# Block attention with two gated layers on one core: keys of half the batch laid side by side, two pairs' means added by a product, a new table of ranks

## The chip, the cores and the metric

The kernel runs on one core of a Trainium2 chip. The metric is the device time of one execution in microseconds. Three runs of the kernel before took 600.68, 600.81 and 597.73 us (median 600.68). One more execution was profiled; it took 599.21 us, of which 597.5 us lie between its first and last instruction (the span).

## The reference

Attention of 2 batches, 8 heads, 768 positions and head size 64, and behind it two feed-forward layers over the 1536 rows of 512 columns. A query sees the keys less than 16 positions away, and beside them 24 block scores: its product with the elementwise maximum of each block of 32 keys, plus ln 32. Both kinds share one softmax; the block weights are multiplied with the block means of the values.

```python
k_sum = k.reshape(B, H, nb, block, D).max(axis=3)      # block = 32, nb = 24
v_sum = v.reshape(B, H, nb, block, D).mean(axis=3)
scores_l = where(|i - j| < 16, scale * q @ k.T, -1e9)
scores_s = scale * einsum('bhsd,bhnd->bhsn', q, k_sum) + log(block)
a = softmax(concat([scores_l, scores_s]))
attn = a @ concat([v, v_sum], axis=2)
x = attn as 1536 x 512
x = (silu(x @ w_gate) * (x @ w_val)) @ w_out           # 512 -> 1536 -> 512
h = x @ w_in                                           # 512 -> 2048
g = where(h >= 1, h, where(h <= -1, 0, (h + 1)**2 / 4))
out = g @ w2_out
```

The weights arrive as 64-bit numbers and are decoded on the chip into 32-bit ones.

## The kernel before, in words

**Order.** No loop fixes the order of the work. The program registers all work as jobs, each with the engines it may run on and an assumed cost on each, a rank, the jobs it needs, and the buffers it takes and gives back. A planner (`Plan.emit`) picks again and again the job with the smallest start plus weighted rank, on the engine that looks cheapest, and emits its instructions. The table `T` holds ranks, leads, and a weight for each kind of engine. So a change of any number in `T`, or of an assumed cost, may move instructions everywhere. Each engine runs its instructions in the order they were emitted, and the loads and stores stand in one line on SP's queue. Where the planner expects TensorE to wait, `bank` puts up to 14 dummy transposes of the identity ahead of the job (L315, below called pads).

**Attention.** Rows are in three chunks of 512: chunk 0 is batch 0, positions 0 to 511; chunk 1 the rest of batch 0 and the first 256 rows of batch 1; chunk 2 the rest. Heads go in pairs (4 pairs, two heads on the two halves of the partitions), positions in segments of 256, each of 4 tiles of 64 queries. A tile's scores have 120 columns: 96 keys around it and 24 block maxima. For batch 0 the steps of a pair are:
- `kp` (L541): keys are transposed by products with the identity, into two banks (80 and 64 partitions, 16 of them twice).
- `kt` (`kprep_out`): four copies put each tile's 96 keys into `kwin`, one window beside another, overlaps written twice. `km` (`kmax`): block maxima by two reductions on DVE. `kc` (`kmax_out`): the 24 maxima are copied behind each of the 12 windows.
- `sc` (L660): 8 products of 64 queries with 120 columns for each segment. They go to four quarters of the array in turn (which head: row half; which tile of two: column half).
- `mx` (L673, mask and maximum), `ex` (L685, on ACT), `su`/`iv`, `no` (L698, on DVE or POOL), `wt` (L706, transposes into `pt`), `pt` (copied into `pT`).
- `vm` (L509): products of values with a small averaging matrix give the block means in `pv`; `vo` copies them, `ve` (`vmean_put`) copies them on 24 partitions behind each window's values in `vall`, for 8 windows at a time in batch 0.
- `av` (L611): 16 products for each segment, `vall` window (120 rows) by `pT`, into `px`; `xh` copies it on (`x`, rounded), `xl` holds the rest (`px` less `x`).

**Weights.** Columns of w_gate and w_val come in packs of two blocks (`load`); `high` (L917) and `low` on ACT or DVE, `bits` (L926, `wb`), `hi` (`wA`, rounded) and `lo` (L956, the rest) decode a pack. The first products need the first pack and `x`, `xl` of pair 0.

**Products.** Each product of the layers is three passes over high and low parts (`mm3`, L1017): `pg`, `pv`, `acc_y` and `pi` of chunk 0, then `qg`, `qv`, `ro`, `qi`, `rz` for chunks 1 and 2 together, in a seven-product form with sums of blocks made by DVE, or by accumulating DMAs on POOL's queue (`SWD`). The last group of `rz` (p = 4) fills two banks `u` of two column halves `z`; the first half of each is copied and stored as soon as it is done, and the planner keeps writes to the second half behind that copy.

Of the kernel before, what the change touches and what calls it, by code (L numbers as in the profile page):

```python
# [25 lines left out]
 'urge': 0.00011346069898928726,  # L26
 'weight': (1.02, 5246.192, 0.325, 0.246),
# [3 lines left out]
 'd': (7426.952, -4102.226),  # L31
 'load': (-416.392, 5468.45),
 'high': (-5467.851, 6761.982),
 'bits': (-4632.926, 1843.592),
 'keep': (-308.073, -3352.145),
 'read': -1167.652,
 'hi': (-17420.635, 2225.546),
 'lo': (-17088.659, -5268.44),
 'head_rank': (-7078.75, -1117.711, -15102.701, -541.927),
 'half_rank': -3059.895,  # L40
 'start': 318.124,
 'unit': 0.87,
 'e0': 435.229,
 'a1': (61.823, 20.151),
 'a2': (189.329, 3.57),
 'x': (-4041.441, 6543.658),
 'first': (-854.098, 2600.892),
 'st_q': (-1384.045, -839.14),
 'st_qt': (1837.901, 4589.592),
 'st_sc': (-5614.707, -2280.841),  # L50
 'st_mx': (-1948.611, -5245.124),
 'st_ex': (4545.125, -695.61),
 'st_iv': (-4062.65, -3165.785),
 'st_no': (3318.58, 1959.608),
 'st_wt': (-144923.789, -442.806),
 'st_pt': (3747.761, 1508.611),
 'st_av': (-5559.373, -4379.57),
 'st_xh': (4195.107, -5.4),
 'st_xl': (-1026.525, -5190.027),
 'kl': (-9172.661, -250.396),  # L60
 'kp': (2952.663, -4662.355),
 'kt': (-2213.424, 261.921),
 'km': (-2717.732, -11590.452),
 'kc': (4577.0, 14734.269),
 'vl': (2791.992, 4670.201),
 'vm': (4107.362, 3808.015),
 'vs': -7497.287,
 'vo': (2313.603, -25934.416),
 've': (1052.554, 4976.716),
 'ql': (-5577.219, -14715.322),  # L70
 'wl': (-2275.937, -19196.435),
 'wide': 4,
 'st_su': (-668.269, 6285.357),
 'seg': (-3459.658, 407.411),
 'ko': (1505.985, 573.628),
 'swd': -3.45,
 'edge': 2,
 'j': 8901.273,
 'jus': 84.768,
 'cap': (19.368, 86.309),  # L80
 'lead': (3.861, 6.562, -15.754, -44.079, 30.375, -21.312, -1.156, -7.677, -5.803, 8.813, 1.459, -43.099, -0.913, 10.89, 0.906, 0.905, -35.721, 38.133, 2.844, 42.453, 40.532, -82.313, 14.043, -46.999, -71.2, 1.812)}


class Plan:
# [17 lines left out]
    WEIGHT = dict(zip(("ACT", "DVE", "DVE+", "POOL", "SWD"), (*T["weight"], T["swd"])))  # L102
# [33 lines left out]
    def emit(self):  # L136
# [14 lines left out]

        def free_at(ring, more=0):
            n = len(used[ring]) + more - self.rings[ring]
            if n < 0:
                return 0.0
            t, left = used[ring][n] if n < len(used[ring]) else (0.0, 1)
            return None if left else t

        while ready:
            best = None  # L160
            for name in ready:
# [15 lines left out]
                for kind, us in engines.items():  # L177
                    engine, port = kind.strip("+"), kind == "POOL" or kind[-1] == "+"
                    start = max(start0, free.get(engine, 0.0))
# [28 lines left out]
            idle = start - free.get(engine, 0.0)  # L208
            free[engine] = start + us
# [39 lines left out]
def tile_block_attention_ffn(  # L249
# [266 lines left out]

    def vmean_put(b, p, i, engine):
# [8 lines left out]
    PARTS = ((0, 80, ((0, 1), (1, 6))), (64, 64, ((7, 4), (11, 1))))  # L526

    def kprep(b, p, *tags):
        n = S // P
        for i, (r0, rows, _) in enumerate(PARTS):  # L530
# [14 lines left out]
    def kprep_out(p, i, engine):  # L545
        pk = pend["pk", p, i]
        r0, _, groups = PARTS[i]
# [9 lines left out]
    def kmax(p):  # L557
        n = PARTS[0][1] * (S // P) // BLOCK
        for i, at, to in ((0, 0, n), (1, n, NB)):
            col = at * BLOCK - PARTS[i][0] * (S // P)  # L560
            nc.vector.tensor_reduce(
                kmaxs[p][:, at:to],
# [37 lines left out]
    def values(c, p, tag, one=None):  # L600
# [3 lines left out]
        for i, (b, s) in enumerate(chunk_segments(c)):  # L604
            if one not in (None, i):
                continue
            pT, vwin = pend.pop(("pT", b, s, p)), vwins[(b * NSEG + s) % 2]
            for w in range(WPS):
                col = i * SEG + w * QT
                for h in range(2):  # L610
                    nc.tensor.matmul(  # L611
                        px[h * D:(h + 1) * D, col:col + QT], vwin[0:KN, w, 2 * p + h],
                        pT[0:KN, 2 * h + w // 2, w % 2 * QT:(w % 2 + 1) * QT],
                        start=True, stop=True,
                    )
# [22 lines left out]
    def stages(b, s, p, wide, first=None):  # L638
# [4 lines left out]
        def scores(*tags):  # L643
# [12 lines left out]
            for w in range(0, WPS, 2):  # L656
                for j in range(2):
                    for h in range(2):
                        head = slice(h * D, (h + 1) * D)
                        nc.tensor.matmul(  # L660
                            scs[h][j * QT:(j + 1) * QT, w // 2],
                            qT[head, (w + j) * QT:(w + j + 1) * QT], kwin[p][head, s * WPS + w + j],
# [57 lines left out]
        ("sc", {"PE": 0.57}, "st_sc", ()),  # L720
# [4 lines left out]
        ("no", {"DVE+": 0.67, "POOL": 1.25}, "st_no", ("iv",)),  # L725
# [5 lines left out]
    def head_jobs(b, p, t, banks, after):  # L731
# [5 lines left out]
        job(("kl", *n), {"DMA": (0.95, 1.65 if b else 1.8, 2) if near else (0.45, 1.55, 1)}, t + T["kl"][b], lambda e, ring: load_k(b, p, ring), (), (("kraw",) if near else ("kraw", "kord"),),  # L737
            after=after)
        keys = ("kl", *n)
        job(kp, {"PE": 0.78 if near else 1.95}, t + T["kp"][b], lambda e, *tags: kprep(b, p, *tags[:2]),  # L740
            [keys] + before, (banks, banks), [(keys, 0)])
        for i, us in enumerate(((0.87, 0.92), (0.69, 0.75))):
            job(("kt", *n, i), dict(zip(("ACT", "DVE"), us)), t + T["kt"][b],
                lambda e, i=i: kprep_out(p, i, e), [kp], (), [(kp, i)])
        job(("km", *n), {"DVE": 0.97}, t + T["km"][b], lambda *_: kmax(p), [kp], (),
            [(kp, 0), (kp, 1)])
        job(("kc", *n), {"DVE+": 0.36, "POOL": 0.7, "ACT": 0.4}, t + T["kc"][b], lambda e: kmax_out(p, e), [("km", *n)] + before)
        if p == 0:
# [13 lines left out]
            job(("vo", b), {"DVE": 0.25, "ACT": 0.27}, t + T["vo"][b], lambda e: vmean_out(b, e),  # L762
                [("vm", b)], (), [(("vm", b, 0) if steps else ("vm", b), 0)])
        for i in range(2 if b else 1):
            job(("ve", *n, i), {"POOL": 0.9, "ACT": 0.62, "DVE+": 0.43} if b else {"POOL": 1.8, "ACT": 1.1, "DVE+": 0.75}, t + T["ve"][b],
# [3 lines left out]
    def step_jobs(c, p, t, banks, after):  # L769
# [4 lines left out]
        job(("ql", *n), {"DMA": (0.96 * len(pieces(c)), 1.08, 2 * len(pieces(c))) if c else (0.45, 0.9, 1)}, t + T["ql"][c > 0], lambda e, ring: load_q(c, p, ring), (),  # L774
            (("s16", "s17") if c else ("s16", "s17", "s14", "s15"),), after=after)
        job(("q", *n), {"PE": 0.42 if c else 1.0}, t + T["st_q"][c > 0], lambda e, tag, _: queries(c, p, tag),
            [("ql", *n)], (banks, ("qT",)), [(("ql", *n), 0)])
        job(("qt", *n), {"DVE": 0.7, "ACT": 0.61}, t + T["st_qt"][c > 0],
# [13 lines left out]
        if not c:  # L792
            for i, (b, s) in enumerate(segs):
                u = t + T["seg"][0] * i
                h = (*n, i)
                job(("av", *(h if not i else n)), {"PE": 0.56},
                    u + T["st_av"][0], lambda e, tag, i=i: values(c, p, tag, i),
                    [("pt", b, s, p), ("ve", b, p, 0), ("wl", b, s)] + ([("av", *n, 0)] if i else []), (banks,),
                    [(("wt", b, s, p), 1)])
                av, xh, xl = (("av", *n), ("xh", *n), ("xl", *n)) if i else (  # L800
                    ("av", *h), ("xh", *h), ("xl", *h))
                job(xh, {"ACT": 0.4, "DVE": 0.42}, u + T["st_xh"][0],
# [27 lines left out]
    def segment_jobs(b, s, p, t, banks, done):  # L830
# [3 lines left out]
        more = {"sc": [("kt", b, p, 0), ("kt", b, p, 1), ("kc", b, p), ("qt", c, p)]}  # L834
# [14 lines left out]
        for name, engines, dt, needs in STAGES:  # L849
            fn = fns[name]  # L850
            if name == "su" and not wide:
                continue
# [938 lines left out]
```

## Time and profile before

| what | value |
|---|---|
| runs | 597.73, 600.68, 600.81 us |
| profiled execution | 599.21 us, span 597.5 us |
| TensorE (PE) busy | 586.8 us, 98% |
| VectorE (DVE) busy | 488.5 us, 82% |
| ScalarE (ACT) busy | 397.8 us, 67% |
| GpSimd (POOL) busy | 107.7 us, 18% |
| share of PE in the chain that ended last | 91% |

PE's busy time counts everything it runs, pads too, and ends of products are modelled; so a window in which PE is all busy may still hold a few tenths lost where it changes from one kind of product to another. The other engines' busy shares say how much room each has, not what they hold up.

### The profile page before, as it was taken

How to read it: one execution, taken by the hardware profiler on the slowest of the kernel's cores; microseconds unless marked ns; L12 is line 12 of the kernel's file. 1: busy time of each engine (PE TensorE's matmuls, PEld its weight loads, DVE VectorE, ACT ScalarE, POOL GpSimd, SP SyncE). 2: the span in 40 equal slices, each digit the busy share in tenths (PEclk: the TensorE clock that was granted, in tenths of full speed). 3: DMA queues.
4: the chain of work that ended last, by engine and by line, in shares of the span. 5: the costliest groups of instructions: out<-in, count | busy, mean ns of one | idle time of the engine just before them, and what ended most of it. 6: DMA issues, size and time to landing. Idle time of an engine off the chain costs nothing.

```text
span 597.5 us, 10820 instructions
## 1 busy us (share of the span) xinstructions
PE 586.8 (98%) x3989; PEld 498.4 (83%) x3989; DVE 488.5 (82%) x885; ACT 397.8 (67%) x734; POOL 107.7 (18%) x133
## 2 busy tenths in 40 slices
PE   8889999999999999999999999999999999999997
PEld 7779888888787778888888888888788788999996
DVE  4888888998887989887877777988988899989850
ACT  4797776674887988664443436577858677887631
POOL 3221000000031110331101001361320121255000
PEclk9999999999999999999999999999999999999999
DMA  8999999998573997998978457999789698999221
GB/s 212 304 325 271 310 328 311 362 360 321 176 259 102 261 292 289 296 210 236 255 209 195 159 159 184 315 232 176 141 207 238 207 194 241 302 233 186 46 71 54
DMA packets 117429, 137.81 MB, mean 231 GB/s; under 512 B 38784, under 2 KB 94080, under 8 KB 117376
## 3 DMA queue, kind: packets, MB, share of 16 engines
q1 hardware_dynamic: 101056, 114.05, 59.8%
q0 software_dynamic: 16320, 23.07, 23.4%
q8 instruction: 31, 0.51, 0.3%
q14 instruction: 22, 0.18, 0.1%
HBM read 91.23 MB, written 28.31 MB: 200 GB/s over the span
## 4 chain that ended last, share of the span: by engine, by line
PE 91%; DMA 3%; DVE 3%; SPq 1%; ACT 1%; issue 0%; POOL 0%; POOLq 0%; DVEq 0%; ACTq 0%
PE rz L1017 14%; PE acc_y L1017 13%; PE ro L1017 10%; PE qv L1017 10%; PE qg L1017 10%; PE qi L1017 9%; PE pi L1017 8%; PE pg L1017 6%; PE pv L1017 6%; PE px L611 2%; DMA sj<-wj 2%; PE sc L660 2%; PE pt L706 1%; DMA raw<-in_moe_w_val_dram 1%; PE pk L541 1%; PE pq L592 1%
## 5 line engine op out<-in xcount | busy, mean ns | idle before, releaser
L1017 PE MATMUL rz<-wr,cells 128*128 128x256 f32 x672 | 81.4, 283 | 0.6 <-ACT ra L408 0.5
L1017 PEld LDWEIGHTS rz<-wr,cells 128*128 128x128 f32 x672 | 81.0, 192 | 1.2 <-ACT ra L408 1.0
L1017 PE MATMUL ro<-cells,wr 128*128 128x512 f32 x252 | 57.9, 390 | 0.0
L1017 PEld LDWEIGHTS ro<-cells,wr 128*128 128x128 f32 x252 | 47.2, 188 | 10.3 <-ACT ru L408 0.6
L1017 PE MATMUL acc_y<-wA,h 128*128 128x512 f32 x192 | 47.6, 395 | 0.0
L1017 PE MATMUL qi<-cells,wjs 128*128 128x512 f32 x192 | 46.3, 389 | 0.0
L1017 PE MATMUL pi<-y,wA 128*128 128x512 f32 x128 | 45.2, 405 | 0.0
L956 DVE TENSOR_TENSOR wA<-wb,wA 128x1024 fp32r<-128x1024 f32 x34 | 42.6, 1256 | 2.4 <-ACT wA L408 1.6
L917 ACT ACTIVATE dd<-raw 128x1024 f32<-128x1024 f32 x34 | 38.8, 1145 | 7.7 <-DMA raw<-in_moe_w_val_dram 5.5
L926 DVE SCALAR_TENSOR_TENSOR wb<-dd 128x1024 int32<-128x1024 int32 x34 | 42.0, 1239 | 2.0 <-ACT dd L408 0.9
L1017 PEld LDWEIGHTS qi<-cells,wjs 128*128 128x128 f32 x192 | 36.0, 188 | 7.5
L1017 PEld LDWEIGHTS acc_y<-wA,h 128*128 128x128 f32 x192 | 35.3, 188 | 7.3 <-issue 0.2
L1017 PE MATMUL qi<-cells,wjo 128*128 128x512 f32 x144 | 35.9, 390 | 0.4 <-DVE qu L1398 0.4
L1017 PE MATMUL qg<-cells,wjs 128*128 128x512 f32 x144 | 35.6, 390 | 0.0
L1017 PE MATMUL qv<-cells,wjs 128*128 128x512 f32 x144 | 35.4, 389 | 0.0
L1017 PE MATMUL acc_y<-h,wA 128*128 128x512 f32 x144 | 35.1, 391 | 0.0
L1017 PE MATMUL pg<-x,wA 128*128 128x512 f32 (+1 forms) x112 | 34.5, 367 | 0.3 <-ACT x L408 0.3
L1017 PE MATMUL pv<-x,wA 128*128 128x512 f32 (+1 forms) x112 | 34.0, 362 | 0.0
L956 DVE TENSOR_TENSOR wjs<-sj,wjs 128x1024 fp32r<-128x1024 f32 x20 | 24.5, 1224 | 10.0 <-ACT wjs L408 9.8
L1017 PEld LDWEIGHTS qi<-cells,wjo 128*128 128x128 f32 x144 | 26.9, 188 | 6.3 <-DVE qu L1398 0.8
L1017 PEld LDWEIGHTS qg<-cells,wjs 128*128 128x128 f32 x144 | 27.0, 188 | 5.8 <-DVE wjs L956 0.2
L1017 PEld LDWEIGHTS qv<-cells,wjs 128*128 128x128 f32 x144 | 27.0, 188 | 5.6
(228 smaller groups left out, 1346.1 us busy)
## 6 DMA issues: line engine op xcount, KB each, us to landing
raw<-in_moe_w_out_dram SPq DMA_DIRECT2D x14, 1024.0 KB, 7.9
raw<-in_moe_w_in_dram SPq DMA_DIRECT2D x16, 512.0 KB, 6.6
raw<-in_moe_w_gate_dram SPq DMA_DIRECT2D x12, 512.0 KB, 7.5
raw<-in_moe_w_val_dram SPq DMA_DIRECT2D x12, 512.0 KB, 8.4
kept_g<-wb SPq DMA_DIRECT2D x12, 512.0 KB, 6.6
wj<-kept_g SPq DMA_DIRECT2D x12, 512.0 KB, 7.7
sj<-kept_g SPq DMA_DIRECT2D x24, 256.0 KB, 4.2
big<-in_v_dram SPq DMA_DIRECT2D x24, 192.0 KB, 4.8
```

Of the source, the lines that this page charges most:

```text
L541: nc.tensor.matmul(cols[h * D:(h + 1) * D, r], kraw[b, p][one, h, r], ident[one, one], start=True, stop=True, skip_group_check=True)
L592: nc.tensor.transpose(pq[:, r * P:(r + 1) * P], raw[:, r].rearrange("p h d -> p (h d)"), ident)
L611: nc.tensor.matmul(px[h * D:(h + 1) * D, col:col + QT], vwin[0:KN, w, 2 * p + h], pT[0:KN, 2 * h + w // 2, w % 2 * QT:(w % 2 + 1) * QT], s ...
L660: nc.tensor.matmul(scs[h][j * QT:(j + 1) * QT, w // 2], qT[head, (w + j) * QT:(w + j + 1) * QT], kwin[p][head, s * WPS + w + j], start=Tru ...
L706: nc.tensor.transpose(pt[0:KN, w * P:(w + 1) * P], v_["sm"][:, w], ident)
L917: nc.scalar.activation(x[:, 0], raws[k][:, :, :, 1].bitcast(F32), AF.Prelu, scale=2.0 ** -112, alpha=2.0 ** 32)
L926: nc.vector.scalar_tensor_tensor(b, x[:, 0], 3, x[:, 1], op0=ALU.logical_shift_left, op1=ALU.bitwise_or)
L956: e.tensor_tensor(out, a, b, op=ALU.subtract)
L1017: nc.tensor.matmul(dst, lhs(a), rhs(b), start=first and i == 0, stop=last and i == 2, **more)
```

## The change

Four things change, and the table of ranks with them.

1. Batch 0's keys are no longer copied into windows. `kprep_out` copies each bank's 384 columns side by side into `lines`; `kmax` writes the 24 maxima behind them, and `kc` is gone for batch 0. The two banks are 64 partitions each. A tile's scores are now two products in the same quarter of the array: 96 keys, then 24 maxima (16 products for each segment in place of 8).
2. For chunk 0 of pairs 0 and 1 (`APART`) the block means aren't copied behind the windows first. A tile `vn` (zero in its first 96 partitions, means in the next 24) is multiplied with all 256 columns of `pT` for each head, and the window products (96 rows) are added to it. `ve` for these two pairs then fills 4 windows, not 8.
3. The last `rz` products are registered as column half 0 of both banks, then column half 1 of both.
4. POOL may now also run `lo`, `gated`, `square`, sums and subtractions that were DVE's (or accumulating DMAs'); two kinds `DVE-` and `DVE=` get weights of their own. Nearly all numbers of `T` are new.

```diff
- 'weight': (1.02, 5246.192, 0.325, 0.246),
+ 'weight': (0.478, 9216.415, 0.434, 0.466, 0.153, 0.189),
...
+    def means_put(p, engine):
+        at = APART.index(p) * 2 * D
+        copy(engine, means[0][KW:KN, at:at + 2 * D], pend["pv", 0][32 * p:32 * p + NB, 0:2 * D])
+
     def vmean_put(b, p, i, engine):
-        n = WPS if b else 2 * WPS
+        n = WPS if b or p in APART else 2 * WPS
...
+    def parts_of_keys(b):
+        return ((0, 64, ()), (64, 64, ())) if b in LINE else PARTS
...
-    def kprep_out(p, i, engine):
+    def kprep_out(b, p, i, engine):
         pk = pend["pk", p, i]
+        if b in LINE:
+            copy(engine, lines[p][:, i * S // 2:(i + 1) * S // 2], pk[:, 0:S // 2])
+            return
...
+            if apart:
+                for h in range(2):
+                    at = (2 * APART.index(p) + h) * D
+                    nc.tensor.matmul(
+                        px[h * D:(h + 1) * D, i * SEG:(i + 1) * SEG], means[0][0:KN, at:at + D],
+                        pT[0:KN, 2 * h:2 * h + 2].rearrange("p x c -> p (x c)"),
+                        start=True, stop=False, skip_group_check=True)
...
+                        if b in LINE:
+                            at = wstart(s * WPS + w + j)
+                            both = ((slice(0, KW), slice(at, at + KW)), (slice(KW, KN), slice(S, S + NB)))
+                            for to_, from_ in both:
+                                nc.tensor.matmul(
+                                    to[:, to_], qs, lines[p][head, from_], start=True, stop=True,
+                                    skip_group_check=True)
+                            continue
...
-        job(("kc", *n), {"DVE+": 0.36, "POOL": 0.7, "ACT": 0.4}, t + T["kc"][b], lambda e: kmax_out(p, e), [("km", *n)] + before)
+        if b not in LINE:
+            job(("kc", *n), {"DVE+": 0.36, "POOL": 0.7, "ACT": 0.4}, t + T["kc"][b], lambda e: kmax_out(p, e), [("km", *n)] + before)
...
-        job(("lo", k), {"DVE+": COST["lo"]["DVE+"]}, t + T["lo"][late(k)], lambda e: lo_pack(k, e), [("hi", k)], (),
+        job(("lo", k), COST["lo"], t + T["lo"][late(k)], lambda e: lo_pack(k, e), [("hi", k)], (),
...
-                steps += [(p, j, x) for x in (every if st == 1 else [(y,) for x in every for y in x])
+                steps += [(p, j, x) for x in (every if st == 1 else [(every[u][z],) for z in range(2) for u in range(2)])
```

PE ahead of the first layer products, in the kernel before (`sc` scores, `pt` transposed weights of the softmax, `pv` with L509 block means, `px` attention's output, `pg` first layer; 128x128 of the identity alone is a pad):

```order
L660 MATMUL sc<-big_78,big_119 64x120 x16
L509 MATMUL pv<-big_119 32x128 x16
L509 MATMUL pv<-vrest,big_119 32x128 x8
L315 MATMUL px<-ident 128x128 x12
L611 MATMUL px<-pT,big_119 64x64 x16
L315 MATMUL px<-ident 128x128 x7
L611 MATMUL px<-pT,big_119 64x64 x16
L1017 MATMUL pg<-x_696,wA 128x256
```

Two pairs' outputs stand here with pads ahead of each, and the first `pg` right behind the second.

The same place in the changed kernel, where L639 is the product with the means and L750 the transposes:

```order
L514 MATMUL pv<-vrest,big_119 32x128 x8
L320 MATMUL px<-ident 128x128 x2
L639 MATMUL px<-pT,vn 64x256 x2
L646 MATMUL px<-pT,big_119 64x64 x8
L639 MATMUL px<-pT,vn 64x256 x2
L646 MATMUL px<-pT,big_119 64x64 x8
L639 MATMUL px<-pT,vn 64x256 x2
L646 MATMUL px<-pT,big_119 64x64 x8
L639 MATMUL px<-pT,vn 64x256 x2
L646 MATMUL px<-pT,big_119 64x64 x8
L320 MATMUL pt<-ident 128x128 x7
L750 MATMUL pt<-ident,big_78 120x128 x8
```

The four segments of pairs 0 and 1 stand together now, and 8 of the transposes of pairs 2 and 3 have moved ahead of the first `pg`.

ACT from the first pack's decoding to the copies of `px`, in the kernel before (`dd` decoding, exponentials L685, `big_119<-big_119` the copies of means behind the windows, `x` the copies of `px`):

```order
L917 ACTIVATE dd<-raw 128x1024
L685 ACTIVATE big_78<-big_78,mx 128x120 x4
L408 ACTIVATE pT<-pt 120x512 x3
L408 ACTIVATE big_119<-pv 128x128
L917 ACTIVATE dd<-raw 128x1024
L408 ACTIVATE dd<-raw 128x1024
L685 ACTIVATE sm_79,big_78<-sm_79,mx 128x120 x4
L408 ACTIVATE big_119<-big_119 24x8x128 x2
L408 ACTIVATE x_696<-px 128x256 x2
L408 ACTIVATE x_709<-px 128x256 x2
```

Both copies of means and two sets of exponentials stand ahead of the copies of `px` here.

The same place in the changed kernel (`vn` the copies of means for pairs 0 and 1):

```order
L973 ACTIVATE dd<-raw 128x1024
L413 ACTIVATE pT<-pt 120x512
L729 ACTIVATE big_78<-big_78,mx 128x120 x4
L413 ACTIVATE vn<-pv 24x128 x2
L413 ACTIVATE big_119<-pv 128x128
L413 ACTIVATE big_119<-big_119 24x4x128 x2
L973 ACTIVATE dd<-raw 128x1024
L413 ACTIVATE dd<-raw 128x1024
L413 ACTIVATE x_723<-px 128x256 x2
L413 ACTIVATE x_732<-px 128x256 x2
L729 ACTIVATE sm_79,big_78<-sm_79,mx 128x120 x4
```

Four exponentials and one copy of `pT` have left the stretch, the copies of means are halved in size, and two small copies into `vn` have come in.

## Rows read from the trace of the kernel before

**Rows 1.** The page: busy time by engine; the chain that ended last, by engine.
```profile
PE 586.8 (98%) x3989; PEld 498.4 (83%) x3989; DVE 488.5 (82%) x885; ACT 397.8 (67%) x734; POOL 107.7 (18%) x133
...
PE 91%; DMA 3%; DVE 3%; SPq 1%; ACT 1%; issue 0%; POOL 0%; POOLq 0%; DVEq 0%; ACTq 0%
```
**Rows 2.** Busy time by stretch: PE, PEld, DVE, ACT, POOL, clock, DMA share, GB/s.
```profile
30.00:60.00 30.00, 27.38 (x306) 24.76 (x305) 25.60 (x64) 26.00 (x65) 5.91 (x6) 1.00 1.05 298
60.00:90.00 30.00, 30.00 (x200) 24.41 (x199) 26.22 (x69) 21.61 (x57) 2.52 (x3) 1.00 1.05 319
...
450.00:480.00 30.00, 29.58 (x131) 24.19 (x130) 25.33 (x38) 23.17 (x37) 3.38 (x3) 1.00 0.78 204
```
**Rows 3.** PE in order of time: start, us, line, tile [idle before <-releaser].
```profile
15.43 0.23 PE L541 MATMUL pk<-ident,kord 80*64 80x80 f32 x1
15.45 0.27 PE L588 MATMUL pq<-ident,qraw 128*64 128x128 f32 x1
...
31.77 0.98 PE L315 MATMUL px<-ident 128*128 128x128 f32 x7
34.65 1.15 PE L611 MATMUL px<-pT,big 120*64 120x64 f32 x32 [1.89 <-ACT big L408]
36.14 0.39 PE L1017 MATMUL pg<-x,wA 128*128 128x256 f32 x1 [0.34 <-ACT x L408]
```
**Rows 4.** The chain that ended last, from 40 us: start, us, what.
```profile
40.35 0.87 PE pt L706 x8
...
42.81 2.02 PE px L611 x64
...
48.14 0.72 PE pg L1017 x6
...
51.45 0.57 PE sc L660 x16
```
**Rows 5.** ACT in order of time, 25 to 37 us.
```profile
25.13 1.20 ACT L917 ACTIVATE dd<-raw 128x1024 f32<-128x1024 f32 x1 [2.42 <-DMA raw<-in_moe_w_val_dram]
26.21 0.39 ACT L685 ACTIVATE big<-big,mx 128x120 f32<-128x120 f32 x1
...
27.73 1.55 ACT L408 ACTIVATE pT<-pt 120x512 f32<-120x512 f32 x3
29.16 0.28 ACT L408 ACTIVATE big<-pv 128x128 f32<-128x128 f32 x1
...
30.85 1.16 ACT L408 ACTIVATE dd<-raw 128x1024 int32<-128x1024 uint32 x1
31.91 0.38 ACT L685 ACTIVATE sm<-sm,mx 128x120 f32<-128x120 f32 x1
...
33.54 2.13 ACT L408 ACTIVATE big<-big 24x1024 f32<-24x1024 f32 x2
35.70 1.21 ACT L408 ACTIVATE x<-px 128x256 fp32r<-128x256 f32 x4
```
**Rows 6.** DVE in order of time: both halves of two packs, and `xl`.
```profile
28.35 1.22 DVE L956 TENSOR_TENSOR wA<-wb,wA 128x1024 fp32r<-128x1024 f32 x1
...
32.04 1.87 DVE L926 SCALAR_TENSOR_TENSOR wb<-dd 128x1024 int32<-128x1024 int32 x1 [0.59 <-ACT dd L408]
...
34.68 1.23 DVE L956 TENSOR_TENSOR wA<-wb,wA 128x1024 fp32r<-128x1024 f32 x1
...
36.12 1.42 DVE L628 TENSOR_TENSOR xl<-px,x 128x256 fp32r<-128x256 f32 x4
```
**Rows 7.** The end, in order of time: PE's weight loads and ACT's copies.
```profile
588.54 4.01 PEld L1017 LDWEIGHTS rz<-wr,cells 128*128 128x128 f32 x33 [0.32 <-ACT ra L408]
...
593.22 0.77 PEld L1017 LDWEIGHTS rz<-wr,cells 128*128 128x128 f32 x6 [0.68 <-ACT ra L408]
593.22 0.97 PE L1017 MATMUL rz<-wr,cells 128*128 128x256 f32 x6 [0.47 <-ACT ra L408]
```
**Rows 8.** POOL in order of time: a subtraction of the layers.
```profile
56.92 1.30 POOL L956 TENSOR_TENSOR h<-u,h 128x512 fp32r<-128x512 f32 x1
```

More of the change, by code (lines that the diff above doesn't have):

```diff
@@ new lines @@
+ 'half_rank': -424.23,
+ 'start': 559.042,
+ 'unit': 0.506,
+ 'e0': 422.878,
+ 'a1': (74.069, 21.997),
+ 'a2': (183.261, 21.332),
+ 'x': (2962.191, -6338.631),
+ 'first': (6168.202, 1133.574),
+ 'st_q': (-5550.855, -349.613),
+ 'st_qt': (-2822.789, -5933.592),
+ 'st_sc': (-4129.389, -2047.311),
+ 'st_mx': (934.53, 433.773),
+ 'st_ex': (6611.948, -5681.133),
+ 'st_iv': (-4707.567, -4306.953),
+ 'st_no': (7610.928, 2185.245),
+ 'st_wt': (-130662.294, -864.398),
+ 'st_pt': (-2099.047, 8242.495),
+ 'st_av': (3867.69, -17386.017),
@@ L100 @@
     SWITCH, LEAD, TILED = 0.11, 0.09, ("sc", "av", "kp", "vm")
-    WEIGHT = dict(zip(("ACT", "DVE", "DVE+", "POOL", "SWD"), (*T["weight"], T["swd"])))
+    WEIGHT = dict(zip(("ACT", "DVE", "DVE+", "POOL", "DVE-", "DVE=", "SWD"), (*T["weight"], T["swd"])))
     def __init__(self, rings):
@@ L150, in emit, with queue @@
         ready = [name for name in jobs if not waits[name]]
+        def queue(engine):
+            return "POOL" if engine == "SWD" else engine
         def free_at(ring, more=0):
@@ L177, in emit @@
                 for kind, us in engines.items():
-                    engine, port = kind.strip("+"), kind == "POOL" or kind[-1] == "+"
-                    start = max(start0, free.get(engine, 0.0))
+                    engine, port = kind.strip("+-="), kind == "POOL" or kind[-1] in "+-"
+                    start = max(start0, free.get(queue(engine), 0.0))
                     if engine == "DMA" or engine == "SWD":
@@ L207, in emit @@
             ready.remove(name)
-            idle = start - free.get(engine, 0.0)
-            free[engine] = start + us
+            idle = start - free.get(queue(engine), 0.0)
+            free[queue(engine)] = start + us
             if port:
@@ L607, in values @@
             pT, vwin = pend.pop(("pT", b, s, p)), vwins[(b * NSEG + s) % 2]
+            apart = not c and p in APART
+            rows_ = slice(0, KW if apart else KN)
+            if apart:
[5 more added lines that the diff above has]
+                        start=True, stop=False, skip_group_check=True)
             for w in range(WPS):
@@ L724, in tile_block_attention_ffn @@
         ("iv", {"DVE": 0.37}, "st_iv", ("ex",)),
[L725 removed]
+        ("no", {"DVE-": 0.67, "POOL": 1.0}, "st_no", ("iv",)),
         ("wt", {"PE": 0.42}, "st_wt", ("no",)),
@@ L850, in segment_jobs @@
             fn = fns[name]
+            if name == "sc" and b in LINE:
+                engines = {"PE": 0.62}
             if name == "su" and not wide:
                 continue
+            if name == "pt" and not c:
+                engines = {"ACT": 0.61, "DVE=": 0.69}
             if wide and name == "ex":
@@ L1188, in use_jobs, with act_jobs @@
                     put_jobs(c, m, t, names[m], acc, UE)
-    def act_jobs(kind, h, src, t, made, held, slots, dve="DVE"):
+    def act_jobs(kind, h, src, t, made, held, slots, inside=False):
+        dve = "DVE-" if inside else "DVE"
         gate = ("u" if h[0] in JOINT else "u2", *h)
@@ L1370, in term_jobs @@
                 lambda e, ring, b=b: term_hi(st, k, b, e, ring), [source, *before], (CELLS,))
-            job(split(b), {"DVE+": 0.7}, LATE,
+            job(split(b), {"DVE-": 0.7, **({} if b == 4 else {"POOL": 1.32})}, LATE,
                 lambda e, b=b: term_lo(st, k, b, e), [("th", st, k, b)], (),
@@ L1564, in stage_rows @@
                     [("rl", *n_)], (("wA",),), follows=prior("gh", ("wh", *n_)))
-                job(("wl", *n_), {"DVE+": cut[2]}, LATE,
+                job(("wl", *n_), {"DVE-": cut[2], **({} if p == 7 else {"POOL": cut[3]})}, LATE,
                     lambda e, a=n_, sign=sign: cut_weight(*a, sign, "lo", e), [("wh", *n_)], (),
```

196 lines of the change are left out of this document (100 added, 96 removed).

## Prediction

> **What bounds the kernel now.** I read the page's busy times and chain first. PE is busy 98% of the span, and 91% of the chain that ended last is its own [rows 1]. So time can come from three places only: work that PE does, time in which PE has nothing it may do, and the two ends. The view by stretches says where PE is idle: 27.38 of 30 are busy from 30 to 60 us, then it fills its windows (30.00); the worst one later is 450 to 480 with 29.58 [rows 2]. Over the whole product part the holes I can name come to about 1.2 us. That is all a better order could win there. The head is different. Between 28 and 37 us PE runs pads and waits: 7 pads of 0.98 us, then 1.89 us for ACT's copy of the means behind the windows (`big`), then 0.34 us for `x` [rows 3]. The first layer product starts at 36.14 us, although the first pack's rest was ready at 28.35 + 1.22 = 29.57 us [rows 6]. So 6.6 us of the head are spent on attention's chain through ACT. At the end PE's weight loads stand still twice, 0.32 and 0.68 us, for ACT's copy `ra` [rows 7].
>
> **The change part by part.**
>
> *The head.* Of ACT's work between the first pack and `x`, I price the new order by the old durations [rows 5]. It starts when the first pack lands, at 25.13 us, in both: the loads ahead of it on SP's queue are the same in number. Decoding takes 26.21 - 25.13 = 1.08, one `pT` (29.16 - 27.73)/3 = 0.48, four exponentials 27.73 - 26.21 = 1.52, two copies into `vn` 2 x 0.28. That makes 28.77 us for the means of pairs 0 and 1, on which `px` waits. Then come the copy of `pv` (0.28), two copies of means at half the size (2.13/2 = 1.06), and the second pack's two decodings (31.91 - 30.85 = 1.06 each): 32.23 us. `x` of pair 0 follows in half of 1.21, at 32.84, pair 1 at 33.44. Before, `x` began at 35.70.
>
> PE in the meantime: `px` for one segment is 32 records (a product of unrounded numbers shows as two), and 64 took 2.02 us [rows 4], so 0.50 us for a segment. The product with the means adds 4 records of 256 columns; at 2.02/64 us for 64 columns, four times that each, 0.50 us. No row shows this product itself. By columns it can't cost less than a rounded 256-column product, 0.72/6 = 0.12 us a record [rows 4], which gives 0.48, and at four times a whole 64-column segment's share it would not pass 1 us; I take 0.50. Four segments from 28.77 are done at 32.8. Behind them stand 7 pads (0.98) and 8 transposes (0.87, rows 4). The first layer product then starts at 34.7 us, not 36.14. That is 1.4 us sooner, with 8 transposes already done that stood later before: 1.4 + 0.9 = 2.3 us. Bounds: nothing, if something else is late; and 4.2 us if PE did not stand behind the pads and transposes (36.14 - 32.84, and the 0.9).
>
> What is late next is DVE. It now makes `xl` of two pairs (1.42 us from 32.9) before the second pack, whose three steps took 34.68 + 1.23 - 32.04 = 3.87 us [rows 6]: ready at 38.2 us. The first pack feeds PE for 24 half products, 24 x 0.12 = 2.9 us, until 37.6. I put 0.3 us on it (from 0 to 0.6). The head wins 2.0.
>
> *Keys and maxima.* The shorter transposes, the dropped window copies and `kc` free some microseconds of DVE and ACT before 22 us. Both then wait for the first pack (ACT idles 2.42 us before it, rows 5), so I count nothing; from 0 to 1 us gained.
>
> *Scores.* A segment's 16 records of 120 columns took 0.57 us [rows 4], 0.036 each. Now 16 of 96 and 16 of 24 run. If columns alone count, that is the same time. If a 24-column record costs as much as one of `px`'s 64-column records (2.02/64 = 0.032), it is 0.8 x 0.57 + 16 x 0.032 = 0.96, so 0.39 more. `px` has two tiles at a time and scores have four, so I halve the record: 0.8 x 0.57 + 0.25 = 0.71, 0.14 more. Eight segments lie in the head, ahead of the wait for the first pack, which covers them. Four lie among the products, where nothing does: 4 x 0.14 = 0.6 us lost (0 to 1.6). [...]
>
> *The end.* PE now turns to the other bank while ACT copies the first half. In the new order at least 6 products (0.7 us at 0.12) lie between the end of a half and the first write behind its copy, and the copy is 0.4 us long. Both waits go. PE's own rows show 0.47 for the second, the loads 0.32 + 0.68 [rows 7]; I take 0.9 (0.6 to 1.0). The last product, copy and store remain as they are.
>
> *The product part.* Attention's pieces cut the products in as many places as before (41 changes to another kind of product in either order), so nothing changes by their number. POOL takes some 27 elementwise operations more and 15 accumulating DMAs less. One costs it 1.30 us [rows 8], against 0.7 on DVE. DVE is 82% busy, POOL 18% [rows 1]; PE stood behind neither for long. A new order may lose as easily as win: between -1.2 (every hole closed) and 27 x 0.6 = 16 us (each extra on PE's path, far off). PE's full windows are the nearest row, so I take +0.3.
>
> The sum: -2.0 + 0.6 - 0.9 + 0.3 = -2.0 us. From the profiled execution's 599.21 (span 597.5, 1.7 around it) that is 597.2. This execution lies 1.5 under the median of the three runs and 0.5 under their mean (599.75). On the mean the sum gives 597.7; I forecast 597.6 us, 0.5% under the median.
>
> **Rivals.**
>
> *DVE takes the head's place.* If the second pack's rest comes 2 us later than I have it, because maxima, a copy of means and `xl` now stand ahead of it on DVE, PE waits at its 25th half product and the head gives nothing. For it: DVE's steps there stand close, and one `wb` took 1.87 us [rows 6]. Against it: the exponentials that fed those steps are done sooner. Time: 599.2 + 0.6 - 0.9 + 0.3, about 599.2, or 600.2 with half the gain at the end lost too; no change.
>
> *One tile, one turn.* Both products of a tile go to the same quarter of the array, one behind the other. If PE starts products strictly in order, the next quarter waits until the 24-column one has started, and scores no longer run four abreast. A transposition of 128 columns on the whole array takes 0.87/8 = 0.11 us [rows 4], so a record of 96 columns 0.08; 16 of them in a row are 1.3 us and the short ones hide or add 0.3: 0.75 to 1.05 us more for a segment, say 0.9. Four among the products lose 3.6. Eight in the head lose 7.2, of which the gap ahead of `px` takes some 3: 4 us late. The time is 599.2 - 2.0 + 3.0 + 4.2 = 604.4 us, slower. It decides from about 0.35 us a segment on. Against it: a `pk` record starts at 15.43, ahead of the last `pq` record at 15.45 that stands before it in the program [rows 3], so a free quarter need not wait for a busy one. [...]
>
> *The new order closes the holes.* With POOL's help DVE is never late, the head wins 3.5: 599.2 - 3.5 + 0.3 - 0.9 - 1.0 = 594.1.
>
> **How the numbers follow.** Forecast 0.50, its own range 595.5 to 599.5; DVE in the head 0.23; one tile one turn 0.15; holes closed 0.12. The whole range goes from 594.0 to 603.0: the third rival's time, and most of the second's. About 0.5% (3 us) is what runs of this kernel, 3 us apart themselves, can tell from no change. Faster than 597.7 are half of the forecast's cases, a little more for the named covers, and all of the holes': 0.28 + 0.12 + a little of the first rival's, 0.42. Slower than 603.7 is most of the second rival's and a tail for a bad order: 0.16. The rest, 0.42, is no change.
>
> **What would show it.** Right: `px` starts near 29 us, the first `pg` near 34.7, no wait of PE's loads for `ra` at the end, scores of a segment at 0.6 to 0.8 us, PE full from 60 us on. Wrong: a `sc` segment over 1.2 us; a gap of PE before its 25th half product ended by DVE `wA`; waits for POOL's `cells`, `h` or `u` in the products.

## The result, and the profile after

The changed kernel takes 604.38 us (median of 6 runs, 603.87 to 605.63), the kernel before 600.13 (median of 6, 597.73 to 600.83): a ratio of 1.0079, 95% interval 1.0058 to 1.0099. It is slower by 0.8%. The forecast was 597.6, and the range ended at 603.0. The span of the profiled execution is 602.7 us, 5.2 more than before.

The page of the changed kernel has the busy time by engine, the queue that brings instructions (packets, MB, share of 16 engines), and the chain:

```profile
PE 588.9 (98%) x4188; PEld 501.1 (83%) x4188; DVE 495.1 (82%) x872; ACT 397.9 (66%) x729; POOL 130.0 (22%) x142
...
q8 instruction: 33, 0.54, 0.4%
...
PE 88%; DVE 4%; ACT 2%; issue 2%; SPq 2%; DMA 2%; POOL 0%; ACTq 0%; DVEq 0%; POOLq 0%
```

Against [rows 1], PE's rows count 199 products more and as many weight loads; 192 of them are those of the scores that were cut in two. The chain has "issue" at 2%, before 0%: time in which an engine waited for nothing that the profile shows. The queue of instructions carried 33 packets, 31 before. What PE waited for, over the whole span (us in total, times, longest):

```profile
PE sc L701 <- issue: 4.6, 3, 2.3
PE pt L320 <- DVE xl L663: 1.0, 1, 1.0
```

The place is shown by PE in order of time, in the head (start, us, line, tile, count, idle before; a row joins neighbouring products of several shapes under the first one's shape). It answers to [rows 3]:

```profile
12.23 1.70 PE L701 MATMUL sc<-big,big 64*64 64x96 f32 x81
14.87 1.00 PE L701 MATMUL sc<-big,big 64*64 64x96 f32 x41 [0.94 <-issue]
...
18.14 0.64 PE L514 MATMUL pv<-big 96*32 96x128 f32 x14
19.12 0.84 PE L514 MATMUL pv<-big 96*32 96x128 f32 x18 [0.34 <-issue]
...
22.28 1.30 PE L701 MATMUL sc<-big,big 64*64 64x96 f32 x53
25.89 0.48 PE L701 MATMUL sc<-big,big 64*64 64x96 f32 x11 [2.31 <-issue]
...
27.31 1.09 PE L614 MATMUL pq<-ident,qraw 128*64 128x128 f32 x16
...
29.80 1.33 PE L701 MATMUL sc<-big,big 64*64 64x96 f32 x56
32.52 0.47 PE L701 MATMUL sc<-big,big 64*64 64x96 f32 x8 [1.39 <-issue]
...
33.94 0.65 PE L639 MATMUL px<-pT,vn 120*64 120x256 f32 x4
34.43 0.64 PE L646 MATMUL px<-pT,big 96*64 96x64 f32 x16
...
38.78 0.98 PE L320 MATMUL pt<-ident 128*128 128x128 f32 x7 [1.02 <-DVE xl L663]
...
40.40 0.36 PE L1073 MATMUL pg<-x,wA 128*128 128x256 f32 x1
```

Runs of scores break off in the middle: 53 products, 2.31 us of nothing, then the 11 that were left. The products behind the gap belong to the same job, and need nothing that the ones ahead of it did not need. The granted clock is 1.00 in every stretch of 5 us up to 45 us here, so the clock has no part in this execution's loss. The first layer product (`pg`) starts at 40.40 us, 36.14 before, 34.7 in the prediction. ACT, in order of time, now waits for PE where [rows 5] show it at work:

```profile
28.45 0.60 ACT L413 ACTIVATE big<-pq 128x512 f32<-128x512 f32 x1 [2.82 <-PE pq L614]
...
33.63 0.56 ACT L413 ACTIVATE vn<-pv 24x128 f32<-24x128 f32 x2 [1.54 <-PE pv L514]
```

The stretches of [rows 2], and one more, 90 to 120 us, in which PE now has a hole; its row of the kernel before stands last:

```profile
30.00:60.00 30.00, 27.52 (x366) 25.02 (x361) 26.56 (x56) 23.71 (x55) 5.15 (x4) 1.00 0.92 257
60.00:90.00 30.00, 30.00 (x268) 24.61 (x267) 25.93 (x48) 12.90 (x26) 2.58 (x2) 1.00 1.00 281
90.00:120.00 30.00, 29.11 (x205) 23.21 (x205) 25.31 (x44) 22.22 (x41) 2.00 (x2) 1.00 1.05 350
450.00:480.00 30.00, 30.00 (x134) 24.85 (x133) 26.79 (x38) 21.46 (x36) 3.38 (x3) 1.00 0.84 234
```
```profile
90.00:120.00 30.00, 30.00 (x136) 24.86 (x135) 26.54 (x32) 18.67 (x22) 0.67 (x1) 1.00 1.00 337
```

The last products run in one piece, and both waits of [rows 7] are gone:

```profile
587.73 11.70 PE L1073 MATMUL rz<-wr,cells 128*128 128x256 f32 x96
```

**The theory.** A product of unrounded numbers is two weight loads and two products in the trace; each of these is called a record here. Counted from the program's start, PE's records and its sequencer's own waits for semaphores together, the four stops of the head stand at 449, 705, 961 and 1217: 256 apart. (Loads and products alone are 446, 696, 950 and 1205; the timeline leaves the waits out.) The instruction queue's packets are 0.54 MB / 33 = 16 KB each. By the trace's DMA records one of them lands ahead of each stop's end, at 13.39, 17.72, 24.38 and 30.95 us, and PE goes on 1.4 to 1.6 us later each time. So PE had used up its instructions and waited for the next 256, called a block below (theory A). Rivals: the short products cost PE time as such (B), or the new order of the other work is what is late (C).

### The profile page after: what moved, and what is told of

The parts are those of the page before. It is cut to its first block, busy times and chain, and to the rows that moved or that the text cites. A ratio compares the mean times of both kernels' runs of the same rounds, so it can differ in the third digit from the quotient of the medians.

```text
span 602.7 us, 11174 instructions
## 1 busy us (share of the span) xinstructions
PE 588.9 (98%) x4188; PEld 501.1 (83%) x4188; DVE 495.1 (82%) x872; ACT 397.9 (66%) x729; POOL 130.0 (22%) x142
## 4 chain that ended last, share of the span: by engine, by line
PE 88%; DVE 4%; ACT 2%; issue 2%; SPq 2%; DMA 2%; POOL 0%; ACTq 0%; DVEq 0%; POOLq 0%
PE rz L1073 13%; PE qi L1073 11%; PE acc_y L1073 11%; PE ro L1073 10%; PE qv L1073 9%; PE qg L1073 9%; PE pi L1073 7%; PE pg L1073 4%; PE pv L1073 4%; DMA raw<-in_moe_w_out_dram 2%; PE pt L750 2%; PE px L646 1%; PE sc L701 1%; PE pk L562 1%; PE sc L705 1%
## 5 line engine op out<-in xcount | busy, mean ns | idle before, releaser
L1012 DVE TENSOR_TENSOR wA<-wb,wA 128x1024 fp32r<-128x1024 f32 x34 | 43.9, 1291 | 2.8 <-ACT wA L413 1.8
L1073 PE MATMUL pi<-y,wA 128*128 128x512 f32 x128 | 43.3, 398 | 0.0
L413 ACT ACTIVATE dd<-raw 128x1024 int32<-128x1024 uint32 x32 | 36.6, 1143 | 0.0
```

What stands on the lines that cost most here:

```text
L413: nc.scalar.activation(out, in_, AF.Copy, scale=scale)
L1012: e.tensor_tensor(out, a, b, op=ALU.subtract)
L1073: nc.tensor.matmul(dst, lhs(a), rhs(b), start=first and i == 0, stop=last and i == 2, **more)
```

## The experiments

**The scores as one product.** In the changed kernel's order:

```
- both = ((slice(0, KW), slice(at, at + KW)), (slice(KW, KN), slice(S, S + NB)))
+ both = ((slice(0, KN), slice(at, at + KN)),)
```

> The changed kernel, in the same order, but each score of batch 0 is one product of 120 neighbouring columns; the block maxima are left out of the scores, so the values are others. Theory A (PE runs out of instructions: it stands still inside runs of scores, with no wait for any engine, 0.94, 2.31 and 1.39 us in the changed kernel, each time 256 weight loads and products after the last stop, and the split doubled the number of these in scores): stops inside scores fall from 4.6 us to under 1.5 us, the first layer product starts 3 to 5 us before 40.40, and the time falls by 3 to 4.5 us, to about 600.5. Theory B (the short products cost PE time as records, 0.14 us a segment): 12 segments by 0.14, 1.7 us less, 602.7, and the stops remain. Theory C (the new order of the other work is what is late): no change, 604.4.

Measured: 597.72 us, 0.998 of before (0.9963 to 0.9996), so 6 us under the changed kernel. The kernel leaves the block maxima out, so its values are not the reference's. No stop is left in scores; the longest stop for "issue" is 0.8 us, in `pk`. PE's start of the means and of the layers:

```profile
28.14 0.65 PE L639 MATMUL px<-pT,vn 120*64 120x256 f32 x4 [0.56 <-ACT vn L413]
...
34.64 0.36 PE L1073 MATMUL pg<-x,wA 128*128 128x256 f32 x1
```

The prediction had 28.77 and 34.7 us. C falls: the order is the same. The gain is larger than A's 3 to 4.5; A and B together give 4.7 to 6.2.

**The split alone.** The kernel before, in its own order:

```
- nc.tensor.matmul(scs[h][...], qT[...], kwin[p][head, s * WPS + w + j], ...)
+ for part in (slice(0, KW), slice(KW, KN)) if b == 0 else (slice(0, KN),):
+     nc.tensor.matmul(scs[h][..., part], qT[...], kwin[p][head, s * WPS + w + j, part], ...)
```

> The kernel before, in its own order and with its own windows of keys; only each score product of batch 0 is cut into one of 96 and one of 24 columns. Theory A (instructions run out): stops without a releaser appear inside runs of scores ahead of 36 us, 2 to 4.5 us in sum, at a distance of 256 records; the first layer product starts 2 to 4 us after 36.14, and the time is 2.5 to 4.5 us longer than before, about 603.5. Theory B (records): 0.14 us a segment, 0.6 to 1.7 us longer, about 601.3, with no stops. Theory C (the order): no change, 600.1.

Measured: 604.36 us, 1.0086 (1.0068 to 1.0104), by this edit alone as much as the whole change loses. The stops, in PE's order of time, then the stretch from 15 to 30 us:

```profile
12.97 1.09 PE L661 MATMUL sc<-big,big 64*64 64x24 f32 x49 [0.37 <-issue]
...
18.57 0.33 PE L541 MATMUL pk<-ident,kord 64*64 64x64 f32 x3 [1.00 <-issue]
...
32.33 0.52 PE L509 MATMUL pv<-big 96*32 96x128 f32 x10 [1.74 <-issue]
```
```profile
15.00:30.00 15.00, 14.00 (x304) 12.45 (x304) 9.54 (x43) 10.59 (x32) 3.77 (x5) 0.77 1.08 296
```

They sum to 3.1 us, at counts 449, 705 and 1217. Two of the three are not in scores, but in `pk` (1.00 us) and `pv` (1.74): the stop falls here on whatever stands at the end of a block. The granted clock was 0.77 in this stretch of this execution, and 8 transposes of `pt` took 1.96 us at 23.65 there, 1.09 before (20.98 in its trace); so part of its 4 us until `pg` (40.28) is the clock's.

**A shift by 64 records.** The changed kernel with this ahead of PE's first work:

```
+ for i in range(16):
+     nc.tensor.matmul(t[:, 0:1], ident, ident[:, 0:1], start=True, stop=True)
```

> The changed kernel with 16 products of one column ahead of everything on PE: 64 weight loads and products more before the first piece of work. Theory A: PE's stops stay at the same count of records from the program's start (449, 705, 961, 1218), so each comes 64 records earlier in attention's work; their sum remains at 3 to 6 us, and the time within 1.5 us of 604.4. Rival (each stop belongs to a piece of work that waits for something the profile doesn't name): the stops stay at the same pieces of work, 64 counts later (513, 769, 1025, 1282).

Measured: 607.07 us (1.0125, 1.0103 to 1.0146); the 16 products took 7.0 us, and the first score starts 4.7 us later than in the changed kernel. PE in order of time:

```profile
16.89 2.48 PE L705 MATMUL sc<-big,big 64*64 64x96 f32 x127
...
26.58 0.74 PE L705 MATMUL sc<-big,big 64*64 64x96 f32 x21
28.00 1.06 PE L705 MATMUL sc<-big,big 64*64 64x96 f32 x43 [0.68 <-issue]
...
33.13 0.77 PE L705 MATMUL sc<-big,big 64*64 64x96 f32 x24
34.44 1.03 PE L705 MATMUL sc<-big,big 64*64 64x96 f32 x40 [0.55 <-issue]
...
40.46 0.56 PE L650 MATMUL px<-pT,big 96*64 96x64 f32 x10 [0.45 <-issue]
```

The run that broke after 53 products now breaks after 21: 32 products, with their loads exactly 64 records, earlier. PE stands still at counts 705 (1.53 us, which the profile puts on DVE), 961, 1217 and 1473. That settles that the count of instructions places the stops here. Those for "issue" sum to 1.7 us, not A's 3 to 6, and the time is 2.7 us over 604.4, not within 1.5. The stop at 449 is gone: its packet had landed at 15.45 us, and PE came there at 17.76. At 705 the packet landed at 20.67 and PE went on at 22.05, as long after it as in the stops above, but DVE's `mx` ended at 21.91 too, so either may have held it. The blocks behind come after 5.95, 6.44 and 6.02 us; they now hold other work, and PE takes longer over some of them. The first row, without a stop, also gives the price of the records: 128 score products in 2.3 us. The kernel before took 1.80 us for 64 of 120 columns (11.41 to 13.21 us), so the split costs 0.12 us a segment.

**The block maxima once for two windows.** The changed kernel, with 128 queries for the short product:

```
+ if j: nc.tensor.matmul(scs[h][:, w // 2, KW:KN], qT[head, w * QT:(w + 2) * QT],
+                        lines[p][head, S:S + NB], ...)
```

> The changed kernel, in the same order; the scores by block maxima of two neighbouring windows are one product (128 queries, 24 columns) in place of two of 64 queries. A segment of batch 0 has 48 weight loads and products in place of 64 (32 in the kernel before). Theory A: half of what the first experiment takes out: stops inside scores fall from 4.6 to 2 to 3 us, and the time by 1.5 to 2.5 us, to about 602.4. Theory B (records): a quarter of the short records' price, 12 segments by 0.07, 0.8 us less. Theory C: no change.

Measured: 631.22 us (1.0522, 1.0482 to 1.0561). All theories missed. PE, two of its turns:

```profile
16.47 0.59 PE L699 MATMUL sc<-big,big 64*64 64x96 f32 x6
16.99 0.62 PE L703 MATMUL sc<-big,big 64*128 64x24 f32 x2
17.54 0.58 PE L699 MATMUL sc<-big,big 64*64 64x96 f32 x2
```

Each turn on a quarter of the array or on a half takes 0.50 to 0.55 us in these rows, of 6 products or of 2, with a granted clock of 0.51 from 15 to 30 us; at the start of the head it takes 0.32 (10.17 to 10.49), with a mean clock of 0.92 from 0 to 15 us. It says nothing on the instructions; it shows what scores look like when they do take turns.

**Blocks with quiet queues.** The kernel before, with 384 products of two sizes on `ident` behind its last one:

```
+ for i in range(48): for j in range(2): for h in range(2):
+     for cols in (slice(0, KW), slice(KW, KN)):
+         nc.tensor.matmul(quiet[h][j * QT:(j + 1) * QT, cols], ident[...], ident[...], ...)
```

> The kernel before, and behind its last product 384 more on PE, 192 of 96 columns and 192 of 24, on the same four quarters as scores, of numbers that lie ready, with nothing to wait for: 1536 weight loads and products, six blocks of 256, while the DMA queues carry only the last stores. In the head of the kernels so far a block was ready 6.0 to 6.8 us after the crossing into the one before it. Theory A1 (the block is late because its packets stand behind the data's): at the end stops every 256 records under 1 us, and the whole tail 14 to 20 us long. Theory A2 (a block takes this long always): a crossing every 6 to 6.8 us, 33 to 40 us in sum, with PE idle more than half of it.

Measured: 617.62 us, one run. PE from 594 us, then one of its stretches:

```profile
594.81 3.11 PE L1764 MATMUL quiet<-ident 64*64 64x96 f32 x161
598.57 2.49 PE L1764 MATMUL quiet<-ident 64*64 64x96 f32 x128 [0.65 <-issue]
602.30 2.49 PE L1764 MATMUL quiet<-ident 64*64 64x96 f32 x128 [1.24 <-issue]
606.03 2.49 PE L1764 MATMUL quiet<-ident 64*64 64x96 f32 x128 [1.24 <-issue]
609.48 2.49 PE L1764 MATMUL quiet<-ident 64*64 64x96 f32 x128 [0.96 <-issue]
612.93 1.93 PE L1764 MATMUL quiet<-ident 64*64 64x96 f32 x95 [0.96 <-issue]
```
```profile
597.00:600.00 3.00, 2.35 (x130) 2.21 (x125) 0.00 (x0) 0.00 (x0) 0.00 (x0) 1.00 0.02 3
```

Nothing but instructions can be late here, and PE stops after every 128 products, 256 records; the first stop stands at count 8385, thirty blocks of 256 behind 705. A block takes 3.45 to 3.73 us from stop to stop with a DMA share of 0.02. In the changed kernel's head the last two took 6.78 (19.11 to 25.89) and 6.63 us, at shares of 1.06 and 0.88. A1 has the better of it: A2's 33 to 40 us are out. But the tail was 20.0 us (to 614.86), at the edge of A1's 14 to 20, and two stops passed 1 us: a block has a time of its own, and some 3 us more in the head, where the queues are busy. The DMA records show where these lie. A packet of the instruction queue takes 1.0 to 1.3 us in the head and 0.9 to 1.3 in the tail, and PE goes on 1.4 to 1.6 us after it has landed in either. But from the end of one stop to the start of the next packet it is 1.1 to 1.5 us in the tail, 4.25 and 3.99 ahead of the head's last two stops (1.7 ahead of the short one of 0.34). The time is lost before the packet starts, as A1 has it.

**One part undone, with a new order.** Windows instead of lines (`LINE = ()`), and means behind the windows again (`APART = ()`):

> The changed kernel with one part undone: keys of batch 0 lie in windows again, with the block maxima copied behind each, and a score is one product of 120 columns. The planner makes a new order for it; means by a product and the order of the last products remain. Theory A (the head's score records make blocks of 256 instructions that PE uses up sooner than the next one comes): 256 weight loads and products fewer ahead of the first layer product; it starts at 34.5 to 36.5 us, stops in scores under 0.5 us, and the time is 597.5 to 599.5, faster than the kernel before by up to 0.4%. Rival (keys side by side saved copies that DVE and ACT now need again, and the order is a poor one): no sooner than 38 us, 601 to 604.

> The changed kernel with the other part undone: the means of two pairs lie behind every window again and no product adds them; the scores remain split. The planner makes a new order. Theory A: the stops in scores remain, 3 to 5 us in sum, and the head loses what the means' product gave: the first layer product at 40 to 42.5 us, the time 604 to 607. Rival (the means' product is what costs, by 16 records of 256 columns, 1.9 us): 602 to 603.

Measured: 605.89 us (1.0098, 1.0068 to 1.0128) and 608.89 (1.0166, 1.0126 to 1.0207). In the first, no stop for "issue" of 0.5 us is left, and `pg` starts at 32.40 us, with less of attention done; but the time is over even the rival's 601 to 604. The planner put in 59 pads where the changed kernel has 28, 14 of them in one place ahead of `pi`:

```profile
154.61 1.69 PE L320 MATMUL pi<-ident 128*128 128x128 f32 x14
```

These 14 take 1.45 us (to 156.06), so 31 more cost up to 3.2; the rest is open. The second, over A's 604 to 607, has stops of 1.8 us in scores and 1.2 in `pv`, and a wait of 3.7 us for `xl` ahead of `pg`. A new order is another kernel: neither run is a clean test of its part. Hence the next one.

**The same order, windows again.** The changed kernel's order, with long copies into windows and the maxima copied by POOL, or by ACT, inside the job of the maxima:

```
-     return ((0, 64, ()), (64, 64, ())) if b in LINE else PARTS
+     return PARTS
+     if b in LINE: kmax_out(p, "POOL")
-     nc.gpsimd.memset(means[0][0:KW], 0.0)
+     nc.vector.memset(means[0][0:KW], 0.0)
```

> The changed kernel in its own order, but keys of batch 0 in windows again (80 and 64 rows transposed, long copies) and the block maxima copied behind each by POOL; a score is one product of 120 columns, all of the reference's work is done. The 96 rows of zeros under the means are set by DVE, not by POOL ahead of the identity. Theory A (score records and PE's stops for instructions make up the loss, not the order): as the kernel whose scores were one product, 597.7, plus what the longer copies cost: 597 to 600; no stop over 0.5 us in scores; the first layer product at 34 to 36 us. Rival (keys side by side are needed by this order, since POOL's copies hold the scores up): the first layer product after 37 us and 601 to 604.

> As the kernel with windows and POOL's copies of the maxima, but ACT makes these copies. ACT waits 2.8 us ahead of the first pack in the changed kernel, so the four copies of 0.4 us may hide there. Theory A: 596.5 to 599.5, up to 1 us sooner than with POOL. Rival (ACT's copies come ahead of its exponentials and delay the first pack): 600 to 602.

> The changed kernel with one line other: the 96 rows of zeros under the means are set by DVE in place of POOL, where they stood 0.46 us ahead of the identity. PE starts at 1.65 in place of 2.11 us. Expected: 0.2 to 0.5 us off the time, 604.1, not to be told from none by the times; the stops for instructions remain, 4 to 6 us in sum.

Measured: with POOL 599.37 us, 0.999 of before (0.9964 to 1.0016); with ACT 599.49, 0.9998 (0.9981 to 1.0015); the line on the zeros alone 603.01, 1.005 (1.003 to 1.007). PE with POOL's copies:

```profile
20.50 1.05 PE L704 MATMUL sc<-big,big 64*64 64x120 f32 x32
...
24.37 0.63 PE L320 MATMUL pt<-ident 128*128 128x128 f32 x4 [0.78 <-DVE mx L736]
...
28.35 0.65 PE L638 MATMUL px<-pT,vn 120*64 120x256 f32 x4 [0.56 <-ACT vn L413]
...
33.26 0.98 PE L320 MATMUL pt<-ident 128*128 128x128 f32 x7 [1.09 <-DVE xl L662]
...
34.87 0.36 PE L1072 MATMUL pg<-x,wA 128*128 128x256 f32 x1
```

With all of the work done, in the same order and with the scores in one piece, the loss is gone: 23.7 us from the first score (11.16) to `pg`, 28.2 in the changed kernel (12.23 to 40.40), 24.7 before (11.41 to 36.14). ACT's copies are no sooner. With zeros on DVE alone PE starts at 1.65 us, and stops of 1.83 and 1.43 us remain, under the 4 to 6 expected; PE was slower ahead of the next stop there (8 transposes took 1.96 us at 21.96, and 1.04 at 28.95; 1.09 at 21.26 in the changed kernel), and it came to that block at 25.56 us without a stop, 2.3 after its packet had landed. The time gained 1.4 us on the changed kernel, more than the 0.2 to 0.5 expected.

**The end alone.** The kernel before with the new order of the last products:

```
- [(y,) for x in every for y in x]
+ [(every[u][z],) for z in range(2) for u in range(2)]
```

> The kernel before with the order of the last products alone changed. The sum on record has 0.9 us for it (0.6 to 1.0): PE's weight loads no longer wait 0.32 and 0.68 us for ACT's copy, and the span is 0.6 to 1.0 us shorter than 597.5, 0.15%, which the times will hardly tell from none. Rival (PE is not released sooner, since another wait or the clock takes the place): nothing.

Measured: 598.94 us, 0.9988 (0.9969 to 1.0008), not told apart from none. The span is 596.8, 0.7 under before. PE's weight loads:

```profile
588.52 2.21 PEld L1017 LDWEIGHTS rz<-wr,cells 128*128 128x128 f32 x18 [0.32 <-ACT ra L408]
591.06 2.21 PEld L1017 LDWEIGHTS rz<-wr,cells 128*128 128x128 f32 x18 [0.32 <-ACT ra L408]
```

The 0.68 has become 0.32, and the products themselves no longer wait; the order of the work ahead decides whether the rest goes too, as in the changed kernel.

**Without pads behind a wait.** The kernel with POOL's copies, and `range(0 if nm == "pt" else plan.pad)`:

> The kernel of the changed order with windows and POOL's copies, without the pads ahead of the transposes of weights (4 and 7 in the head, 1 later). There they stand behind a wait for DVE (0.78 us for the minima, 1.09 us for the rest of x) and ahead of transposes whose data are ready: 11 by 0.117 us, 1.3 us of PE's path. Theory: the first layer product starts 0.8 to 1.3 us before 34.87, and the time is 0.5 to 1.5 us under 599.4, at 0.998 of the kernel before or less. Rival (the transposes wait for something else, or PE's clock falls without them): no change, or longer by up to 2 us with a granted clock under 1.0 ahead of 45 us.

Measured: 598.49 us, 0.9974 (0.9952 to 0.9995): the fastest that does all of the work, by its interval just under the kernel before, and not told apart from the 599.37 with the pads. PE:

```profile
27.90 1.09 PE L749 MATMUL pt<-ident,sm 128*120 128x128 f32 x8 [0.98 <-POOL sm L741]
...
36.48 1.06 PE L749 MATMUL pt<-ident,big 128*120 128x128 f32 x8 [1.18 <-DVE xl L662]
...
37.29 0.36 PE L1072 MATMUL pg<-x,wA 128*128 128x256 f32 x1
```

`pg` came later, not sooner, since the first score did too (14.55 us). From there to `pg` it is 22.7 us, 1.0 less than with the pads.

## Why the prediction was wrong

**The step that failed** is in *Scores*: "Eight segments lie in the head, ahead of the wait for the first pack, which covers them." There was no such wait any more: even with whole scores ACT turned to the first pack at 24.23 us without waiting for it. The split put 256 records into the head, 4 for each of 8 products of 8 segments, one whole block, and PE itself became the last to come: ACT waited 2.82 us for it ahead of the copy of the queries that precedes the decoding, and 1.54 ahead of the means. The prediction counted columns and records on the engine, and took the supply of instructions as given. The trace of before already had a stop, at count 705 like the second one of the changed kernel, which I did not follow up:

```profile
20.20 0.85 PE L541 MATMUL pk<-ident,big 64*64 64x64 f32 x21 [0.56 <-issue]
```

**The size.** From the first score to `pg`, the changed kernel takes 4.5 us more than the same order with whole scores. The parts give it: stops of 4.98 against 0.19 us, 8 segments by 0.12 = 1.0 us, less the waits for others that PE then has instead (2.43 against 1.02): 4.79 + 1.0 - 1.4 = 4.4.

**The head term came out with whole scores, in part by luck.** The means were to be multiplied at 28.77 us and `pg` to start at 34.7: 28.35 and 34.87 were measured with POOL's copies. ACT began on the first pack 0.9 us sooner than the 25.13 assumed, and then its copy of `pT` waited 0.53 us for PE. The four segments were done at 32.2 us, not 32.8, and then PE waited 1.09 us for DVE's `xl`, which the sum does not have. The prediction gives `px` 32 records for a segment; it is 16, since `av` is 8 products there and not 16, and 0.50 us is what 16 of the 64 take. The means' product takes 0.44 to 0.49 us a segment (33.94 to 34.43 is the first), predicted 0.50. DVE's second pack makes no wait: PE has none at all from 34 to 60 us in that kernel.

**The price of a short record** was well sized: 0.12 us a segment, 0.14 predicted. It was the smaller part.

**The end.** Both waits are gone in the changed kernel, as forecast. The gain of 0.9 us itself is too small for the times to show.

**The product part** was a second miss. Without the split's 0.6 the sum has 2.6 us of gain, but the same order with whole scores gained 0.6 by its ratio (from a gain of 2.2 to a loss of 1.0). The head's 2 us are there, so the rest went behind `pg`. From there to the end it was 561.4 us before. Less 0.9 for the end and 0.8 for 8 transposes done ahead, that leaves 559.7 with whole scores, and 560.2 with four split segments. The profiles have 561.7 with POOL's copies, 560.2 in the first experiment and 562.3 in the changed kernel: 0.5 to 2.1 us more, where 0.3 was forecast. One hole is named, in 90 to 120 us, where PE waits 0.58 us for DVE. These are single executions, so what the order costs there is not settled.

**The rivals.** "One tile, one turn" came nearest in time (604.4), and by the wrong mechanism: it asked for 0.9 us more a segment, and 0.12 was measured (128 products in 2.3 us, four segments, against 1.80). "DVE takes the head's place" fell with the row of no wait behind `pg`, though DVE's `xl` did hold PE by 1.0 to 1.1 us ahead of it. "The new order closes the holes" fell with 90 to 120 us.

Open: what an instruction packet waits for before it starts in the head. The busy queues are the likeliest reason; no run changes them alone.

## What to carry to other kernels

Where PE works in many small products, count its instructions too: an unrounded product was four in these traces, and 256 of them had to last as long as the next block took to come, here 3.5 to 3.7 us with quiet queues and 6.0 to 6.8 us with busy ones. The sign was an "issue" gap in the middle of a run of like products (2.31 us behind 53 of 64). A distance of 256 between such gaps, PE's waits counted too, and stops that stayed at their counts when 64 records were put ahead, were the proof. Cutting a product in two was not free, though the columns were the same in sum and the quarters of the array too: 0.12 us a segment, and stops of 4.98 us against 0.19.

## What was not expected of the hardware

The stops themselves: up to 2.31 us, at a distance of 256 weight loads, products and waits of PE, and up to 1.24 us with a DMA share of 0.02.

Turns of products on a quarter and on a half of the array took 0.32 us each, of 6 products or of 2, at the start of the head (mean granted clock 0.92 from 0 to 15 us) and 0.50 to 0.55 at 0.51 (631 us for the kernel).

A product of one column on the whole array was no cheaper than a transposition there: 16 unrounded ones, 32 records, took 7.0 us, 0.22 each, and the 14 pads right behind 3.2 us, 0.23 each.

The first 96 products of `pk` took 4.2 us in the changed kernel (5.29 to 9.53) and 2.8 in the one with whole scores and no maxima (5.29 to 8.11), which has the same ones; in windows they took 4.5 us before (4.80 to 9.26) and 6.6 without pads (4.81 to 11.36), all with a granted clock of 1.00. The runs don't show what sets it; it moves whole profiles by 2 to 4 us, which is why the head is measured above from the first score.
